# Stores of the split weights moved from SyncE's transfer queue to ScalarE's, placed by the order's model

## The chip, the cores and the metric

The kernel runs on one core of one Trainium2 chip. The metric is the device time of one execution in microseconds (us); lower is better. The core's engines are TensorE (PE, with its weight loads as PEld), VectorE (DVE), ScalarE (ACT), GpSimd (POOL) and SyncE (SP). Transfers between DRAM and the on-chip memory are issued by SP, ACT or POOL, each through a queue of its own; an issue appears as SPq, ACTq or POOLq in the profile. The transfers of all queues are carried by the core's 16 DMA engines.

## The reference

Two branches are computed from the same layer-normalised input and multiplied: attention over 2048 rows with 32 heads of width 18, and a bilinear gated feed-forward block of inner width 4608.

```python
x = A_x                                       # 1 x 2048 x 576
xn = _layernorm(x, axis=-1)
s = _A_ref(xn, A_wqkv, A_wo)                  # softmax attention, then @ wo
g = _silu(_B_ref(xn, B_w_gate, B_w_up, B_w_down))
...
# _B_ref: h = (x @ w_gate) * (x @ w_up); h @ w_down
```

The result is the product of s and g.

## The kernel before

The matmuls run in a 32-bit format of reduced precision (fp32r), so each operand is split in two: a high part, which is the value rounded to that format, and a low part, which is the rest. The terms that matter of the product of two split operands are added up in PSUM. Splitting the raw feed-forward weights is what this case is about.

The time has three parts. A prologue, to about 194 us, normalises the input, transposes it and makes queries, keys and values. The main loop, to about 2490 us, interleaves the feed-forward block with the attention, so that PE always has something to do. The tail makes the output projection and the product.

The feed-forward block goes over 72 units: 4 chunks of 512 rows (`c`), and for each 18 column blocks of 256 inner columns (`q`). A unit needs two tiles of up and gate weights (`wgu`, one for each n) and one of down weights (`wd`). In the first pass (c = 0, about 194 to 731 us) these tiles are made from raw weights. `g_raw` (L116) loads raw up and gate weights into `wraw`; three calls of `piece` copy the high part on ACT (L193) and subtract it on POOL (L194). `d_raw` (L124) and two calls of `dpiece` (L226 on ACT, L227 on POOL) do the same for the down weights. When a tile is done, `end` stores it to DRAM (`swg` at L199, `swd` at L232), and starts the raw load after next (wgu) or the next one (wd). Passes 2 to 4 load the split tiles from `swg` (L185) and `swd` (L220), in the opposite direction of columns in every other pass. One store of `swd`, at L216, belongs to the last column block and is made in the second pass.

A unit's up product is copied from PSUM on ACT (L680, `us`), multiplied with the gate product on DVE (L687) and split on ACT (L690, `hs`) and POOL (L691). The swapped halves of it are loaded as `hx` (L709), and L719 is the matmul with the down weights, added up on DVE (L747). The attention's scores are computed twice: L596 into the two banks `pa`, from which DVE takes the rows' maximum (L598), and L628 into the two banks `pb`, which ACT turns into exponentials (L630, `pt`). L639 multiplies them with the values. The heads' queries and keys come from DRAM as `pair` and `ring` (L245). The input's columns of the next chunk come as `xc` (L368, L371).

Instructions keep, on each engine and in each queue, the order in which the program issues them. In the main loop that order comes from a planner, `order()`. It keeps two clocks for PE (`clk`, one for each of two rows of PE), a time at which each other engine is free (`free`; `engine(eng, start, taken)` books a piece of work), and a model of the transfer queue (`moved()`). In each turn it takes the next matmul, score or other piece that can go. `small(now)` takes the next piece of split work from the list `chores` when the engine that it starts on is about free.

Of the kernel before, what the change touches and what calls it, by code (L numbers as in the profile page):

```python
# [20 lines left out]
FT = mybir.dt.float32  # L21
# [19 lines left out]
def kernel(  # L41
# [10 lines left out]
    nc = tc.nc  # L52
# [24 lines left out]
    swg = dram.tile([2 * NF2, 128, 18, 128], FT, name="swg")  # L77
    swd = dram.tile([NF2, 128, 2, 2, 2, HALF], FT, name="swd")
# [48 lines left out]
    def g_tile():  # L127
        return wpool.tile([128, 18, 128], FR, name="wgu", bufs=2)

    def d_tile():  # L130
        return wpool.tile([128, 2, 2, 2, HALF], FR, name="wd", bufs=1)
# [5 lines left out]
    def chore(all=True):  # L137
        q = (all and chores) or later
        if q:
            f, a = q.pop(0)  # L140
            f(*a)
# [5 lines left out]
    def ready(done, key):  # L147
        while key not in done:
            assert chores or later
            chore()  # L150
# [7 lines left out]
    def columns_of(u):  # L158
        c, q = units[u]
        return NF2 - 1 - q if c % 2 else q  # L160

    graw, gw, draw, dw = {}, {}, {}, {}
    gdone, ddone = set(), set()

    def g_load(n):
        if n < 2 * NF2:
            graw[n] = g_raw(n)

    def g_get(n):

        if n == 2 * len(units):
            u = n // 2 - 1
            dw[u] = wpool.tile([128, 2, 2, 2, HALF], FR, name="wdl", tag="wgu", bufs=2)
            nc.sync.dma_start(dw[u].bitcast(FT), swd[columns_of(u)])
            ddone.add(u)
        if n >= 2 * len(units):
            return
        f = 2 * columns_of(n // 2) + n % 2
        if n > 1 and n // 2 % NF2 == 0:
            gw[n] = gw[n - 2]  # L180
            gdone.add(n)
            return
        w = gw[n] = g_tile()
        if n >= 2 * NF2:
            nc.sync.dma_start(w.bitcast(FT), swg[f])  # L185
            gdone.add(n)
            return
        if n not in graw:
            ready(gdone, n - 2)
        raw = graw.pop(n)  # L190

        def piece(b):
            nc.scalar.activation(w[:, b:b + 3, :], raw[:, b:b + 3, :], AF.Copy)  # L193
            nc.gpsimd.tensor_tensor(w[:, 9 + b:12 + b, :], raw[:, b:b + 3, :], w[:, b:b + 3, :].bitcast(FT),  # L194
                                    op=OP.subtract)

        def end():
            gdone.add(n)
            nc.sync.dma_start(swg[f], w.bitcast(FT))  # L199
            g_load(n + 2)  # L200

        chores.extend([(piece, (b,)) for b in (0, 3, 6)] + [(end, ())])

    def d_load(n):
        if n < NF2:
            draw[n] = d_raw(n)

    def d_get(n):
        if n >= len(units) - 1:
            return  # L210
        p = columns_of(n)
        if n and n % NF2 == 0:
            dw[n] = dw[n - 1]
            ddone.add(n)
            if n == NF2:
                nc.sync.dma_start(swd[p], dw[n].bitcast(FT))  # L216
            return
        w = dw[n] = d_tile()
        if n >= NF2:
            nc.sync.dma_start(w.bitcast(FT), swd[p])  # L220
            ddone.add(n)
            return
        raw = draw.pop(n)

        def dpiece(k):
            nc.scalar.activation(w[:, k, :, 0, :], raw[:, k], AF.Copy)  # L226
            nc.gpsimd.tensor_tensor(w[:, k, :, 1, :], raw[:, k], w[:, k, :, 0, :].bitcast(FT), op=OP.subtract)  # L227

        def end():
            ddone.add(n)  # L230
            if p < NF2 - 1:
                nc.sync.dma_start(swd[p], w.bitcast(FT))  # L232
            d_load(n + 1)

        chores.extend([(dpiece, (k,)) for k in range(2)] + [(end, ())])
# [342 lines left out]
    with ExitStack() as mid:  # L578
# [225 lines left out]
        def begin():  # L804
            lo.extend(stk.tile([128, S], FR, name=f"o{k}", tag=tag) for k, tag in enumerate(("pair0", "pair1", "ring")))
            loads.extend((fetch_o, (k, c), 0.262) for c in range(2) for k in range(3))
# [86 lines left out]
        clk, free = [0.0, 0.0], {"DVE": 0.0, "ACT": 0.0, "POOL": 0.0}  # L893
# [10 lines left out]
        def engine(eng, start, taken):  # L904
            free[eng] = max(free[eng], start) + taken
            return free[eng] + TAIL[eng]
# [8 lines left out]
        def moved(start, size):  # L915

            queue[0] = max(queue[0], start) + size / 0.24
            return queue[0] + 2.0

        due, rows_done = [], {}  # L920
        there, queue = {}, [0.0]
        na = nb = 0
# [79 lines left out]
        def small(now):  # L1002

            q = chores or later
            if q and q is later and (now < quiet[0] or later[0][0].__name__ in ("second", "inverse") and nb < TOTAL):
                return
            if q:
                steps = KINDS.get(q[0][0].__name__, ())
                eng = steps[0][0] if steps else "POOL"
                if eng == "POOL" or free[eng] <= now + 0.1 + (0.15 * (now - quiet[0]) if q is later else 0.0):  # L1010
                    at = now
                    for eng, taken in steps:
                        at = engine(eng, at + 0.05, taken)
                    if not chores:
                        quiet[0] = now + PAUSES.get(q[0][0].__name__, 6.0)
                    chore()
# [93 lines left out]
        def order():  # L1110
# [5 lines left out]
            while any(heads) or na < TOTAL or nb < TOTAL or due:  # L1116
                now = max(clk)
                small(now)
                if nb == TOTAL and not lo:
                    begin()  # L1120
                if loads and queue[0] <= now + 0.3:
                    f, a, size_mb = loads.pop(0)
# [70 lines left out]

        heads, stuck, parts, loaded, stacks = [], [False], {}, {}, []
        order()


# [115 lines left out]
```

## Time and profile before

| What | Value |
|---|---|
| time of 3 runs, median | 2568.7 us |
| the three runs | 2567.2, 2568.7, 2570.92 us |
| profiled execution, its own time | 2567.59 us |
| profiled execution, span | 2565.8 us |
| mean clock granted to PE | 0.999 |
| PE / PEld busy | 2544.8 / 2106.5 us |
| DVE / ACT / POOL busy | 1931.5 / 1465.2 / 593.3 us |
| bytes moved by DMA | 504.58 MB, of which SP's queue (q1) 487.58 MB |

The span is the time between the first and the last instruction that the profiler saw; the execution's own time has 1.8 us beside it. Busy times are those in which the engine worked on at least one instruction. The profile names a group of instructions by its line in the kernel, its engine, its operation and what it writes and reads, as in `pt<-pb`. Where an engine was idle ahead of an instruction, "<-" gives what ended the wait.

### The profile page before, as it was taken

To read this page: it belongs to the slowest core of one execution; us is meant where nothing else is said; L and a number is where in the kernel's file an instruction comes from. 1 tells how busy PE (TensorE), PEld (TensorE's weight loads), DVE (VectorE), ACT (ScalarE), POOL (GpSimd) and SP (SyncE) were. 2 spreads that over 40 slices of the span, in tenths; PEclk is the share of its full clock that TensorE was granted. 3 is DMA by queue.
4 is the path that set the end of the run, shared out by engine and by line. 5 is a ranking of instruction groups with operands and counts; after the bars stand their busy time and mean duration, and the time that the engine had idled before them with its cause. 6 is when DMAs were issued, how large, how long until landed. Compare 5 with 4: busy or idle time off the path is not lost.

```text
span 2565.8 us, 59206 instructions
## 1 busy us (share of the span) xinstructions
PE 2544.8 (99%) x24360; PEld 2106.5 (82%) x24360; DVE 1931.5 (75%) x3377; ACT 1465.2 (57%) x2688; POOL 593.3 (23%) x663
## 2 busy tenths in 40 slices
PE   8999999999999999999999999999999999999999
PEld 7899888878878888878888888887888888878879
DVE  6208778777778898777778888777888887877537
ACT  5222666666756665655565666555665655555651
POOL 3214334433421111111111111111111111111125
PEclk9999999999999999999999999999999999999999
DMA  7799988888886666565676666665676666664577
GB/s 248 233 283 279 259 227 226 233 222 224 221 193 187 176 180 180 172 182 168 181 186 171 179 175 185 179 166 169 180 192 166 178 184 178 175 177 145 154 203 253
DMA packets 196058, 504.58 MB, mean 197 GB/s; under 512 B 58144, under 2 KB 116384, under 8 KB 156876
## 3 DMA queue, kind: packets, MB, share of 16 engines
q1 hardware_dynamic: 185100, 487.58, 68.2%
q0 software_dynamic: 9952, 11.74, 1.7%
q8 instruction: 192, 3.15, 0.6%
q10 hardware_dynamic: 736, 1.47, 0.2%
q14 instruction: 78, 0.64, 0.1%
HBM read 312.21 MB, written 107.61 MB: 164 GB/s over the span
## 4 chain that ended last, share of the span: by engine, by line
PE 97%; DVE 1%; DMA 1%; SPq 0%; issue 0%; ACT 0%; POOL 0%; DVEq 0%
PE pg L675 34%; PE pg L639 17%; PE pg L719 16%; PE pa L596 12%; PE pb L628 8%; PE pg L402 2%; PE pa L348 2%; PE pb L348 2%; PE pg L1243 1%; PE pa L1243 1%; PE pb L1243 1%; DMA hx<-hs 0%; DMA ring<-sqk 0%; DVE mx L598 0%; DMA xin<-in_A_x_dram 0%; DMA sot<-oc 0%
## 5 line engine op out<-in xcount | busy, mean ns | idle before, releaser
L598 DVE TENSOR_REDUCE mx<-pa 128x1 f32<-128x512 f32 x2048 | 1368.9, 687 | 226.1 <-PE pa L596 113.1
L630 ACT ACTIVATE pt<-pb 128x512 f32<-128x512 f32 x2048 | 1160.8, 597 | 538.2 <-PE pb L628 463.5
L675 PE MATMUL pg<-xc,wgu 64*128 64x512 f32 x7776 | 1363.9, 388 | 0.2 <-DVE acc L747 0.2
L675 PEld LDWEIGHTS pg<-xc,wgu 64*128 64x128 f32 x7776 | 1049.4, 184 | 41.4 <-DVE acc L747 0.5
L628 PE MATMUL pb<-pair,ring 64*128 64x512 f32 x2005 | 780.8, 395 | 2.3 <-DMA ring<-sqk 2.3
L596 PE MATMUL pa<-pair,ring 64*128 64x512 f32 x2006 | 777.3, 393 | 1.8 <-DVE mx L598 1.8
L719 PE MATMUL pg<-wd,hs 64*128 64x288 f32 x3408 | 585.1, 293 | 2.4 <-DVE acc L747 2.4
L719 PE MATMUL pg<-wd,hx 64*128 64x288 f32 x3360 | 572.4, 293 | 2.0 <-DMA hx<-hs 2.0
L719 PEld LDWEIGHTS pg<-wd,hs 64*128 64x128 f32 x3408 | 491.8, 185 | 7.1 <-DVE acc L747 2.8
L691 POOL TENSOR_TENSOR hs<-us,hs 128x512 fp32r<-128x512 f32 x144 | 185.9, 1291 | 1315.7 <-ACT hs L690 1301.6
L719 PEld LDWEIGHTS pg<-wd,hx 64*128 64x128 f32 x3360 | 480.4, 185 | 5.6 <-DMA hx<-hs 2.3
L639 PE MATMUL pg<-pt,vt 128*32 128x512 f32 x4096 | 455.8, 595 | 0.8 <-DVE acc L747 0.6
L596 PEld LDWEIGHTS pa<-pair,ring 64*128 64x128 f32 x2006 | 364.8, 184 | 70.7 <-issue 52.8
L628 PEld LDWEIGHTS pb<-pair,ring 64*128 64x128 f32 x2005 | 364.2, 184 | 9.3 <-issue 2.7
L639 PEld LDWEIGHTS pg<-pt,vt 128*32 128x32 f32 x4096 | 125.6, 110 | 285.1 <-issue 280.0
L747 DVE TENSOR_TENSOR acc<-acc,pg 128x288 f32<-128x288 f32 x544 | 234.0, 446 | 21.1 <-PE pg L719 20.1
L645 DVE TENSOR_TENSOR oc<-oc,pg 128x512 f32<-128x512 f32 x69 | 47.1, 683 | 216.6 <-PE pg L639 213.0
L690 ACT ACTIVATE hs<-us 128x512 fp32r<-128x512 f32 x144 | 91.0, 632 | 149.6 <-DVE us L687 148.0
L194 POOL TENSOR_TENSOR wgu<-wraw,wgu 128x384 fp32r<-128x384 f32 x108 | 108.4, 1015 | 97.3 <-ACT wgu L193 81.3
L643 ACT ACTIVATE oc<-pg 128x512 f32<-128x512 f32 x32 | 19.1, 598 | 184.9 <-PE pg L639 184.9
L687 DVE TENSOR_TENSOR us<-pg,us 128x512 f32<-128x512 f32 x144 | 98.4, 683 | 29.0 <-PE pg L675 22.3
L618 POOL DMA_DIRECT2D pair<-mt x128 | 77.6, 612 | 166.6 <-DVE mt L613 162.5
(143 smaller groups left out, 1366.5 us busy)
## 6 DMA issues: line engine op xcount, KB each, us to landing
wgu<-swg SPq DMA_DIRECT2D x102, 1152.0 KB
hx<-hs SPq DMA_DIRECT2D x140, 512.0 KB
wd<-swd SPq DMA_DIRECT2D x50, 1152.0 KB
swg<-wgu SPq DMA_DIRECT2D x36, 1152.0 KB
pair<-sqk SPq DMA_DIRECT2D x192, 144.0 KB
ring<-sqk SPq DMA_DIRECT2D x384, 72.0 KB
swd<-wd SPq DMA_DIRECT2D x18, 1152.0 KB
sqk<-hl SPq DMA_DIRECT2D x32, 512.0 KB
```

What stands on the lines that cost most here:

```text
L194: nc.gpsimd.tensor_tensor(w[:, 9 + b:12 + b, :], raw[:, b:b + 3, :], w[:, b:b + 3, :].bitcast(FT), op=OP.subtract)
L348: nc.tensor.matmul(p, wq[b, a], xcs[c][:, e, :], start=n == 0, stop=n == len(PAIRS) - 1)
L596: nc.tensor.matmul(p, q[rows, t * 128:(t + 1) * 128], k[rows, c * 512:(c + 1) * 512], start=True, stop=True)
L598: nc.vector.tensor_reduce(mx[h][:, t, c:c + 1], p, axis=AX.X, op=OP.max)
L628: nc.tensor.matmul(p, k[rows, t * 128:(t + 1) * 128], q[rows, c * 512:(c + 1) * 512], start=True, stop=True)
L630: nc.scalar.activation(pt[t, c], p, AF.Exp, scale=scale)
L639: nc.tensor.matmul(p[32 * c:32 * c + 32, :], vt[h // 2][:, t, 6 * (h % 2):6 * (h % 2) + 32], pt[t, c], start=t == ts[0], stop=t == ts[-1])
L675: nc.tensor.matmul(ps, gw[n][half[r], a, :], xg[i][half[r], e, :], start=k == 0, stop=k == len(TERMS) - 1)
L687: nc.vector.tensor_tensor(h32, ps, h32, op=OP.mult)
L691: nc.gpsimd.tensor_tensor(hj[:, 1, :], h32, hj[:, 0, :].bitcast(FT), op=OP.subtract)
L719: nc.tensor.matmul(ps[:, 0:HALF], (hx if k else hs)[u][half[r], j, a, s * 128:(s + 1) * 128], dw[u][half[r], k, j, e, :], start=n == 0, st ...
L747: nc.vector.tensor_tensor(a, a, ps[:, 0:HALF], op=OP.add)
```

## The change

The 53 stores of split tiles (36 of `swg`, 17 of `swd`, 1152 KB each) are no longer issued by SP at the place where the tile is finished. `end` puts them on a list, `saves`. At the head of each turn of `order()`, each new store gets a due time, the time at which the model has POOL free, plus 0.4 us; and when the first store of the list is due and ACT is nearly free in the model, ACT issues it, and the model books 0.5 us on ACT. The store at L216 stays on SP.

```diff
-    graw, gw, draw, dw = {}, {}, {}, {}
+    graw, gw, draw, dw, saves = {}, {}, {}, {}, []
...
         def end():
             gdone.add(n)
-            nc.sync.dma_start(swg[f], w.bitcast(FT))
+            saves.append((swg[f], w.bitcast(FT)))
             g_load(n + 2)
...
             if p < NF2 - 1:
-                nc.sync.dma_start(swd[p], w.bitcast(FT))
+                saves.append((swd[p], w.bitcast(FT)))
             d_load(n + 1)
...
+        save_at = []
...
             while any(heads) or na < TOTAL or nb < TOTAL or due:
                 now = max(clk)
                 small(now)
+                while len(save_at) < len(saves):
+                    save_at.append(free["POOL"] + 0.4)
+                if saves and save_at[0] + max(0.0, free["ACT"] - now - 0.1) <= now:
+                    save_at.pop(0)
+                    nc.scalar.dma_start(*saves.pop(0))
+                    engine("ACT", now, 0.5)
```

In the changed kernel the stores are at L1124. The following rows give the program's order on one engine: line, operation, what is written and read, the shape, and in brackets the semaphores that the row waits for. DMAHW0 to DMAHW7 are eight counters that the transfers of SP and ACT take in turn, in the order of the program; an issue waits on its counter until the transfer that took it before has landed.

ACT at the start of the main loop, before: the last copies of the prologue (`vo`), then the first unit's `us` and `hs`.

```order
L408 ACTIVATE vo_1164<-pg 128x16x18 [waits DMAHW0_49,PE_49]
L408 ACTIVATE vo_1164<-pg 128x16x18 [waits PE_49]
L680 ACTIVATE us<-pg 128x512 [waits PE_49]
L690 ACTIVATE hs<-us 128x512 [waits DVE_49]
L193 ACTIVATE wgu<-wraw 128x384 [waits DMAHW5_49,PE_49,Pool_49]
```

The same place now:

```order
L408 ACTIVATE vo_1164<-pg 128x16x18 [waits DMAHW7_49,PE_49]
L408 ACTIVATE vo_1164<-pg 128x16x18 [waits PE_49]
L1124 DMA swg<-wgu 128x2304 [waits DMAHW2_49,Pool_49]
L1124 DMA swd<-wd 128x2304 [waits DMAHW7_49,Pool_49]
L1124 DMA swg<-wgu 128x2304 [waits DMAHW2_49,Pool_49]
L680 ACTIVATE us<-pg 128x512 [waits PE_49]
L690 ACTIVATE hs<-us 128x512 [waits DVE_49]
L193 ACTIVATE wgu<-wraw 128x384 [waits DMAHW4_49,PE_49]
```

Three stores that SP issued during and right after the prologue stand together ahead of the first `us`; the third waits on the same counter, DMAHW2, that the first one takes, since that is used again between them.

ACT in a unit of the middle of the first pass (about 650 to 656 us before), before: exponentials (`pt`), the gate's copies, and the next split.

```order
L226 ACTIVATE wd<-draw 128x2x288 [waits DMAHW4_49,DMAHW2_49]
L630 ACTIVATE pt<-pb 128x512 [waits PE_49] x4
L680 ACTIVATE us<-pg 128x512 [waits PE_49,Pool_49]
L630 ACTIVATE pt<-pb 128x512 [waits PE_49] x4
L690 ACTIVATE hs<-us 128x512 [waits DVE_49]
L630 ACTIVATE pt<-pb 128x512 [waits PE_49]
L193 ACTIVATE wgu<-wraw 128x384 [waits DMAHW4_49,DMAHW5_49,DMAHW3_49,Pool_49]
```

The same place now:

```order
L226 ACTIVATE wd<-draw 128x2x288 [waits DMAHW4_49,DMAHW2_49]
L680 ACTIVATE us<-pg 128x512 [waits PE_49]
L630 ACTIVATE pt<-pb 128x512 [waits PE_49]
L1124 DMA swg<-wgu 128x2304 [waits DMAHW7_49,Pool_49]
L630 ACTIVATE pt<-pb 128x512 [waits PE_49] x2
L690 ACTIVATE hs<-us 128x512 [waits DVE_49]
L630 ACTIVATE pt<-pb 128x512 [waits PE_49] x2
L1124 DMA swd<-wd 128x2304 [waits DMAHW5_49,Pool_49]
L630 ACTIVATE pt<-pb 128x512 [waits PE_49] x2
L193 ACTIVATE wgu<-wraw 128x384 [waits DMAHW6_49,DMAHW0_49]
```

Two stores stand between exponentials, each with a wait for POOL and for a counter, and the exponentials are spread otherwise about `us` and `hs`.

SP at the same place, before: the raw loads, `hx`, and the stores among them.

```order
L199 DMA swg<-wgu 128x2304 [waits DMAHW1_49,Pool_49]
L116 DMA wraw<-in_B_w_up_dram 64x9x128 [waits DMAHW2_49]
L116 DMA wraw<-in_B_w_gate_dram 64x9x128 [waits DMAHW3_49]
L709 DMA hx<-hs 64x2048 [waits DMAHW4_49,PE_49]
L709 DMA hx<-hs 64x2048 [waits DMAHW5_49]
L232 DMA swd<-wd 128x2304 [waits DMAHW6_49,Pool_49]
L124 DMA draw<-in_B_w_down_dram 64x2x288 [waits DMAHW7_49]
```

The same place now:

```order
L709 DMA hx<-hs 64x2048 [waits DMAHW1_49,PE_49]
L709 DMA hx<-hs 64x2048 [waits DMAHW2_49]
L116 DMA wraw<-in_B_w_up_dram 64x9x128 [waits DMAHW3_49,Pool_49]
L116 DMA wraw<-in_B_w_gate_dram 64x9x128 [waits DMAHW4_49]
L124 DMA draw<-in_B_w_down_dram 64x2x288 [waits DMAHW5_49,Pool_49]
```

Both stores are gone from SP; their wait for POOL now stands on the raw loads behind them, and `hx` goes ahead of the raw loads here.

## The prediction

> **What bounds the kernel now.** I read the page's busy times first, then the chain that ended last, then the busy time by stage, and last the waits and the order of time on the engines that the change touches.
>
> ```profile
> span 2565.8 us, 59206 instructions
> PE 2544.8 (99%) x24360; PEld 2106.5 (82%) x24360; DVE 1931.5 (75%) x3377; ACT 1465.2 (57%) x2688; POOL 593.3 (23%) x663
> ...
> PE 97%; DVE 1%; DMA 1%; SPq 0%; issue 0%; ACT 0%; POOL 0%; DVEq 0%
> ```
>
> TensorE works for 99% of the span and carries 97% of the chain. The change removes no matmul, so its gain can only come out of the idle 21 us (2565.8 - 2544.8) and out of a clock below 1, and only where the stores run, in the first pass (194 to about 731 us). The table by stage shows where that pass loses time at all. Its columns are the window, its length, the busy time of PE, PEld, DVE, ACT and POOL with counts, the granted clock, the DMA share and GB/s.
>
> ```profile
> core 0: us, PE busy (x) PEld busy (x) DVE busy (x) ACT busy (x) POOL busy (x), PEclk, DMA share, GB/s
> ...
> 200.00:240.00 40.00, 40.00 (x369) 36.89 (x367) 36.90 (x62) 11.40 (x23) 19.71 (x18) 1.00 1.05 285
> 240.00:260.00 20.00, 19.23 (x204) 18.50 (x203) 18.71 (x34) 7.76 (x15) 12.46 (x13) 1.00 1.03 262
> 260.00:280.00 20.00, 17.96 (x157) 17.12 (x155) 12.40 (x21) 9.87 (x20) 6.98 (x6) 0.91 0.97 266
> ...
> 740.00:760.00 20.00, 17.72 (x145) 13.74 (x145) 13.65 (x22) 11.46 (x20) 6.55 (x7) 0.91 0.84 185
> ```
>
> Two stages stand out. In 260 to 280 us PE idles 20.00 - 17.96 = 2.04 us, and the clock of 0.91 takes another 0.09 x 20 = 1.8: 3.8 us. In 740 to 760 us it is 2.28 + 1.8 = 4.1 us. Together 7.9 us, 0.3% of the time, is nearly all that better transfers could win. What ended the two idle times stands in the waits of PE between 179 and 770 us (total, times, longest), and in the chains of these two stages and of the whole (start, us, what):
>
> ```profile
> PE pb L628 <- DMA ring<-sqk: 2.3, 1, 2.3
> PE pg L719 <- DMA hx<-hs: 2.0, 1, 2.0
> ```
>
> ```profile
> 1.66 4.47 DMA xin<-in_A_x_dram
> ...
> 263.62 10.87 DMA hx<-hs
> ...
> 745.33 10.38 DMA ring<-sqk
> ```
>
> Both are loads from SP's queue that were late: hx, issued at 263.62 us, landed 10.87 us later, and a ring load took 10.38, where the first transfer of the kernel, with nothing ahead of it, took 4.47.
>
> **The change, part by part.** SP loses 53 stores (36 of swg, 17 of swd). Their own time on SP, from the views of the two lines (least, median, longest ns, first and last start), and SP's waits in 179 to 770 us:
>
> ```profile
> L199 SPq DMA_DIRECT2D swg<-wgu x36: 326/343/3736, 153.4 to 705.5; - x36
> ```
>
> ```profile
> L232 SPq DMA_DIRECT2D swd<-wd x17: 326/1226/3704, 179.5 to 712.8; - x17
> ```
>
> ```profile
> SPq L199 <- POOL wgu L194: 97.8, 25, 10.6
> ...
> SPq L199 <- DMA swd<-wd: 11.2, 5, 3.3
> SPq L232 <- POOL wd L227: 9.8, 6, 2.3
> SPq L245 <- DMA draw<-in_B_w_down_dram: 7.9, 20, 1.1
> ```
>
> The issues free 36 x 0.343 + 17 x 1.226 = 33 us of SP's time, spread over 540 us. The 97.8 and 9.8 us that SP stood waiting for GpSimd are not won: in the new order the raw loads L116 and L124, which followed the stores, carry that wait themselves, since they overwrite the raw tile that GpSimd reads. So SP gets ahead by its issue times, and that counts only where a late load holds PE.
>
> Stall 1, hx at 263.62. SP's order there:
>
> ```profile
> 260.27 0.35 SPq L199 DMA_DIRECT2D swg<-wgu  x1
> ...
> 262.78 0.74 SPq L116 DMA_DIRECT2D wraw<-in_B_w_gate_dram  x1
> 263.62 2.28 SPq L709 DMA_DIRECT2D hx<-hs  x2
> 266.02 1.98 SPq L232 DMA_DIRECT2D swd<-wd  x1
> ```
>
> The swg store was issued 3.35 us ahead of hx in the same queue and leaves that queue. If hx then comes at least 2.0 us sooner, the stall goes, for -3.8 us. But the store's 1.18 MB go over the same 16 engines at the same time, and these are busy for 0.97 of the stage, so 0 is the other end; a loss I leave out here, as no new byte is added. Another queue beside SP's is in the trace: GpSimd's stores sot of 36 KB, and what each queue moved in the whole span:
>
> ```profile
> sot<-oc POOLq DMA_DIRECT2D x20, 36.0 KB, 6.1
> ```
>
> ```profile
> q10 hardware_dynamic: 736, 1.47, 0.2%
> ```
>
> From 284 to 715 us those stores land in a median of 6.1 us, well short of the 10.87 that hx takes behind SP's own backlog, so a second queue does not stand behind the first. I take -1.5, a little under the middle, for the share of 0.97. The Trainium skill, "DMA: Bandwidth & Descriptors", section "Queues, rings and completion order", says that each engine alternates between the queues that have work, a packet from one and then from the other. By it hx would gain nothing: in 10.87 us at 266 GB/s 2.9 MB pass, of which the store is 1.18; if the 1.7 MB of SP's queue alternate with the store's 1.18, all but some 0.5 MB are shared evenly, and the last byte of hx still lands after 2.9 MB. The sum would then be 1.5 us higher. The row of sot agrees with the alternation as such, but a small transfer is not hx, so I keep the middle.
>
> Stall 2, ring at 745.33. Ahead of it SP does, at the end of the pass:
>
> ```profile
> 712.80 1.23 SPq L232 DMA_DIRECT2D swd<-wd  x1
> ...
> 742.12 5.71 SPq L245 DMA_DIRECT2D ring<-sqk  x6
> ```
>
> The last moved store ends 28 us before the six ring loads start, and between them stand raw loads and the loads of the next chunk's xc, which stay. What SP gains is this issue, 1.23 us, and perhaps its wait. The ends are -4.1 (2.3 us sooner, the stall gone) and +0.5 (the loads meet other transfers); I take -1.0, the issue time, since PE is then held 1.2 us less, less a little for the transfer.
>
> ScalarE gets 53 issues. What one costs there is shown by the only transfers it issues now, L795; how its exponentials L630 stand to the matmuls L628, from the orders of time of ACT and PE:
>
> ```profile
> L795 ACTq DMA_DIRECT2D wor<-in_A_wo_dram x4: 388/446/1190, 2483.5 to 2485.7; - x4
> ```
>
> ```profile
> 2483.53 0.63 ACT L690 ACTIVATE hs<-us 128x512 fp32r<-128x512 f32 x1 [0.41 <-DVE us L687]
> 2483.53 2.59 ACTq L795 DMA_DIRECT2D wor<-in_A_wo_dram  x4
> ```
>
> ```profile
> 339.06 1.10 ACT L630 ACTIVATE pt<-pb 128x512 f32<-128x512 f32 x2
> ```
>
> ```profile
> 338.36 0.39 PE L628 MATMUL pb<-pair,ring 64*128 64x512 f32 x1
> ...
> 339.95 0.39 PE L628 MATMUL pb<-pair,ring 64*128 64x512 f32 x1
> ...
> 340.40 0.39 PE L628 MATMUL pb<-pair,ring 64*128 64x512 f32 x1
> ```
>
> There are two pb banks. The two exponentials end at about 339.63 and 340.16; the matmuls that take their banks again start at 339.95 and 340.40, so the slack is 0.24 to 0.32 us, and I use 0.3. What holds ACT for longer while an exponential is next holds PE by the rest. An issue of 0.446 is 0.15 beyond that, 53 x 0.15 = 8 us, if nothing covers it; but the issue starts with the ACTIVATE ahead of it (both 2483.53) whose 0.63 us covers it, and the order's model books 0.5 us on ACT for it. The other end of the issue time is SP's for the same stores: 36 x 0.04 + 17 x 0.93 = 17 us. I take a tenth of the 8, +0.75, range 0 to +17.
>
> The holds are the dearer part. A store on ACT waits for GpSimd's subtraction and, since all these transfers share eight counters in turn, for the transfer eight issues back. Queued behind it on ACT are exponentials (PE's pb banks), the split pieces L193 and L226 (GpSimd, then PE's weights) and the gate's copies L680 and L690 (DVE, GpSimd, then hx). GpSimd's end is booked with 0.4 us to spare, so I charge the counters. Nothing of the kind is on ACT today; the nearest rows are SP's. A typical one is L245 behind draw: 7.9 / 20 = 0.4 us, 0.1 beyond the slack. From 284 to 715 us, where exponentials run, there are 41 stores:
>
> ```profile
> swg<-wgu SPq DMA_DIRECT2D x27, 1152.0 KB
> swd<-wd SPq DMA_DIRECT2D x14, 1152.0 KB
> ```
>
> So 41 x 0.1 = 4, of which ACT's busy share of 57% meets work that is ready: +2.3. The low end is 0 (the transfer eight back has landed each time). The high end is the row of L199 behind swd, 11.2 / 5 = 2.24 us each, 1.94 beyond the slack; ten such are 19 us.
>
> At the loop's start three stores that SP issued from 153.4 us on wait until the loop begins and are issued together on ACT, and the third waits for the first to land. ACT's next work is
>
> ```profile
> 200.59 0.60 ACT L680 ACTIVATE us<-pg 128x512 f32<-128x512 f32 x1 [5.92 <-PE pg L675]
> ```
>
> ACT is free from 200.59 - 5.92 = 194.7. With a landing in 4.47 us (the least above) and an issue of 0.45 it is free again at 199.6 and nothing is late; with 10.87 at 206.0, and us, hs and the first hx come 5.4 us later. PE is busy for all of 200 to 240 us and has other columns to work on, so I take +1, from -1 (the stores no longer crowd the prologue's loads) to +5.
>
> Sum against the profiled execution of 2567.6 us (span 2565.8 and 1.8 around it): 2567.6 - 1.5 - 1.0 + 0.75 + 2.3 + 1.0 = 2569.2, say 2569.0. The median of the runs shown is 2568.7, 1.1 above the profiled one, and 0.2% of it, about what a measurement of this kernel can tell from no change, is 5.1 us.
>
> **The rivals.** A is the forecast: SP's 33 us were never on the path, the terms cancel, 2569.
>
> B, faster: both loads arrive in time, -3.8 and -4.1, and ACT's terms stay near 1: 2567.6 - 7.9 + 1 = 2561. For it: two stalls on late SP loads are all that PE lacks, and sot's 6.1 us. Against: stall 2 is 28 us past the last store, and the DMA share near stall 1 is 0.97.
>
> C, slower: ACT is held by the counters as SP was. Five of 36 stores waited 2.24 us each; of 53 it would be 7.4, so seven at 1.94 beyond the slack: +13.6, and 2567.6 - 2.5 + 0.75 + 1.0 + 13.6 = 2580. It decides when the holds beyond the slack pass about 7 us (5.1, the 1.1 between the profiled time and the median, and the 2.5 that the stalls give back, less 1.75 of the other terms), that is four such holds. For it: SP keeps its stock of ring, pair and raw loads in flight, so the one eight back is often only some microseconds old, and ACT had no such wait. Against: SP's five stood behind swd, which leaves SP's queue, and ACT is idle for 43% of the span.
>
> A further way, not a case of its own: the stores land later because ACT issues them later, and the next split L193 waits for its wgu tile. The next pass reads them from DRAM only after the raw loads of this one end, so only that tile counts, and it is within C.
>
> The Trainium skill, the same page, section "Issuing engines are not separate DMA queues", says that issuing from more engines saves only the sequencer's issue time. Case A says the same from the DMA share of 0.97, so it moves no chance.
>
> **How the numbers follow.** A 0.45, B 0.22, C 0.33: B can win at most 7.9 us and must win two thirds of it, C has the wider bounds. These are also the chances of within 0.2%, faster and slower. The likeliest is 2569.0, its own range 2563.6 to 2573.8. For 8 times in 10 the range takes in most of B (down to 2562) and of C (up to 2584, eight holds and an early stretch at +3); a tenth is left out above, where the 17 and 19 us ends meet, and less below.
>
> **What would show it.** In the profile after, q10 should move 1.47 + 53 x 1.18 = 64 MB, and the SP rows of L199 and L232 be gone. Stall 1: PE's wait for hx shrinks to below 1 us and the clock of 260 to 280 us is above 0.91. Stall 2: PE's wait for ring is still there, about a microsecond shorter. Holds: ACT's stores show times of 0.4 to 0.5 us, and waits behind DMA on ACT's queue of 5 to 15 us in sum; the idle time of PE L628 behind ACT, which has no row now, is 1 to 4 us. Start: L680 begins at 199 to 204 us. It would be wrong if L628 waits on ACT for more than 7 us, or if hx and ring both lose their rows and nothing takes their place.

## The result: slower by 0.7%, and the profile after

The changed kernel takes 2588.22 us (median of 5 runs, 2583.78 to 2591.56), the kernel before 2569.31 us (5 runs). The ratio is 1.0074, with a 95% interval of 1.0063 to 1.0086: 19 us slower, above the range of the prediction. The profiled execution of the changed kernel (span 2589.8 us) is one of its longer ones, 3.3 us above its median.

From the page of the changed kernel, busy times, queues, and the group of the matmuls that feed the exponentials:

```profile
PE 2555.4 (99%) x24360; PEld 2109.4 (81%) x24360; DVE 1929.9 (75%) x3377; ACT 1464.1 (57%) x2688; POOL 593.3 (23%) x663
...
q10 hardware_dynamic: 8368, 64.00, 6.6%
...
L628 PE MATMUL pb<-pair,ring 64*128 64x512 f32 x2005 | 782.4, 396 | 9.6 <-ACT pt L630 6.8
```

The change did what it says: ScalarE's queue q10 now moves 64.00 MB. New is the last row: L628 stands idle behind the exponentials of ACT for 6.8 us; before, its only idle time of 2.3 us was behind a ring load. The table by stage, with the columns of the one before:

```profile
200.00:220.00 20.00, 18.96 (x147) 15.93 (x144) 16.54 (x26) 5.01 (x10) 8.29 (x8) 1.00 0.89 315
...
260.00:280.00 20.00, 15.88 (x132) 14.76 (x130) 11.59 (x18) 10.31 (x18) 7.12 (x6) 0.95 1.06 274
280.00:300.00 20.00, 19.03 (x182) 17.63 (x182) 13.74 (x25) 10.64 (x20) 7.15 (x6) 0.87 0.96 255
...
560.00:580.00 20.00, 18.86 (x201) 17.11 (x199) 17.20 (x30) 16.06 (x32) 6.72 (x7) 1.00 0.72 225
...
600.00:620.00 20.00, 18.75 (x195) 12.88 (x192) 14.11 (x29) 10.99 (x21) 13.26 (x16) 1.00 0.48 152
...
660.00:680.00 20.00, 17.37 (x166) 15.30 (x163) 14.28 (x24) 12.97 (x26) 9.03 (x9) 0.91 0.78 238
680.00:700.00 20.00, 17.56 (x153) 11.88 (x154) 11.83 (x24) 8.08 (x15) 9.89 (x13) 0.91 0.60 171
...
760.00:780.00 20.00, 17.23 (x138) 12.87 (x139) 12.10 (x20) 10.38 (x18) 6.14 (x7) 0.91 0.85 187
```

Counted as in the prediction (idle time of PE, and the missing clock times 20 us), the lost time is:

| Stage, us | before | after | what PE waits for, after |
|---|---|---|---|
| 200 to 220 | 0 | 1.0 | L596 behind DVE |
| 260 to 300 | 3.8 | 8.7 | hx, then an exponential |
| 560 to 580 | 0 | 1.1 | an exponential |
| 600 to 620 | 0 | 1.3 | wd (GpSimd), mainly |
| 660 to 700 | 0.2 | 8.7 | two exponentials |
| 740 to 780 | 4.1 | 4.6 | ring |
| sum | 8.1 | 25.4 | |

The difference is 17.3 us. The medians are 19 us apart, but the two profiled executions counted here 24.0 (2591.56 and 2567.59), so the count places about 70% of it. Some 2 us more are lost from 800 to 2520 us, most of it in one spell of lower clock at 2514 us; the rest this count does not place. Both late loads are still there. PE's waits from 179 to 790 us:

```profile
PE pb L628 <- ACT pt L630: 6.8, 4, 2.6
PE pg L719 <- DMA hx<-hs: 4.1, 1, 4.1
PE pb L628 <- DMA ring<-sqk: 2.8, 1, 2.8
```

The four waits behind ACT end at 299, 564, 670 and 693 us. They take 6.8 us, and the lower clock of the stages 660 to 680 and 680 to 700 us takes 3.6 more: 10.4 of the 17.3 us. The late hx, with the clock behind it, takes 3.9 us more than before.

**What held the exponentials.** ACT's order of time around three stores (start, us; in brackets the idle time ahead and what ended it):

```profile
205.60 0.33 ACTq L1124 DMA_DIRECT2D swg<-wgu  x1
205.98 0.60 ACT L680 ACTIVATE us<-pg 128x512 f32<-128x512 f32 x1 [10.16 <-DMA swg<-wgu]
...
665.14 1.07 ACT L630 ACTIVATE pt<-pb 128x512 f32<-128x512 f32 x2
669.37 0.33 ACTq L1124 DMA_DIRECT2D swd<-wd  x1
669.75 1.08 ACT L630 ACTIVATE pt<-pb 128x512 f32<-128x512 f32 x2 [3.54 <-DMA draw<-in_B_w_down_dram]
...
688.07 1.08 ACT L630 ACTIVATE pt<-pb 128x512 f32<-128x512 f32 x2
692.37 0.33 ACTq L1124 DMA_DIRECT2D swg<-wgu  x1
692.74 2.28 ACT L630 ACTIVATE pt<-pb 128x512 f32<-128x512 f32 x4 [3.59 <-POOL wgu L194]
```

The first is the start, where the third store waits for the first to land. At 669 us ACT stands still for 3.5 us because the store's counter is held by a draw load, one of those which SP issued from 663.12 us on. At 692 us it waits for GpSimd's last subtraction, which was itself behind GpSimd's pair transfers, and these had waited for DVE (SP's order of time, then POOL's):

```profile
663.12 3.44 SPq L124 DMA_DIRECT2D draw<-in_B_w_down_dram  x4
```

```profile
688.78 2.54 POOL L618 DMA_DIRECT2D pair<-mt  x4 [2.78 <-DVE mt L613]
691.34 1.00 POOL L194 TENSOR_TENSOR wgu<-wraw,wgu 128x384 fp32r<-128x384 f32 x1
```

I laid each of the 53 stores beside the times at which its counter and GpSimd's count arrived in the trace. 13 were held for more than 0.3 us after the instruction ahead of them on ACT had ended: 7 by a counter (28.8 us together, the start's 9.3 among them), 6 by GpSimd (9.7 us). The other 40 were not held. At each of the 7 the store starts 0.07 or 0.08 us after its counter's transfer has landed. Only four of the 13, the stores at 298, 563, 669 and 692 us (three held by a counter, one by GpSimd, for 1.8 to 3.2 us), have a wait of L628 behind them. The three longest, 9.3 us at the start, 6.2 at 282 us and 4.8 at 234 us, have none.

The issue itself is cheap, for swd (326 ns in the median) as for swg:

```profile
L1124 ACTq DMA_DIRECT2D swg<-wgu x36: 326/327/382, 195.5 to 732.1; - x36
```

**What made hx later.** The two issues of hx on SP (least, median, longest ns, first and last start), before and after, the stores on ACT's queue, and the matmul that waited:

```profile
L709 SPq DMA_DIRECT2D hx<-hs x2: 596/1119/1642, 263.6 to 265.3; - x2
```

```profile
L709 SPq DMA_DIRECT2D hx<-hs x2: 708/2209/3710, 265.7 to 269.4; - x2
```

```profile
260.94 0.33 ACTq L1124 DMA_DIRECT2D swg<-wgu  x1
...
265.07 0.33 ACTq L1124 DMA_DIRECT2D swd<-wd  x1
```

```profile
279.54 0.60 PE L719 MATMUL pg<-wd,hx 64*128 64x288 f32 x1 [4.12 <-DMA hx<-hs]
```

hx is there at 279.5 us, 13.9 us after its issue at 265.67, against 10.87 before. That is 5.0 us later than before: 2.05 since it is issued later, 2.07 since SP needs 3.71 instead of 1.64 us for the first of the two issues, and 0.9 from the second issue to the landing. What lengthens the issue is not shown. On SP's queue one of the two stores, that of swd, stood behind hx (266.02 against 263.62 us); now it was issued 0.6 us ahead of hx on a queue of its own.

### The profile page after: what moved, and what is told of

Read it like the earlier page. It is cut to its first block, busy times and chain, and to the rows that moved or that the text cites. A ratio compares the mean times of both kernels' runs of the same rounds, so it can differ in the third digit from the quotient of the medians.

```text
span 2589.8 us, 59220 instructions
## 1 busy us (share of the span) xinstructions
PE 2555.4 (99%) x24360; PEld 2109.4 (81%) x24360; DVE 1929.9 (75%) x3377; ACT 1464.1 (57%) x2688; POOL 593.3 (23%) x663
## 4 chain that ended last, share of the span: by engine, by line
PE 71%; DVE 1%; DMA 0%; SPq 0%; issue 0%; ACT 0%; ACTq 0%
PE pg L675 26%; PE pg L639 14%; PE pg L719 13%; PE pa L596 9%; PE pb L628 7%; PE pg L1250 1%; PE pa L1250 1%; PE pb L1250 1%; DMA ring<-sqk 0%; DVE mx L598 0%; DVE mm L610 0%; SPq L245 0%; DVE us L687 0%; DVE acc L747 0%; DVE tp L655 0%
## 5 line engine op out<-in xcount | busy, mean ns | idle before, releaser
L628 PE MATMUL pb<-pair,ring 64*128 64x512 f32 x2005 | 782.4, 396 | 9.6 <-ACT pt L630 6.8
L596 PE MATMUL pa<-pair,ring 64*128 64x512 f32 x2006 | 779.2, 394 | 2.9 <-DVE mx L598 2.9
L596 PEld LDWEIGHTS pa<-pair,ring 64*128 64x128 f32 x2006 | 365.3, 185 | 72.7 <-issue 53.6
L628 PEld LDWEIGHTS pb<-pair,ring 64*128 64x128 f32 x2005 | 365.0, 185 | 19.0 <-ACT pt L630 10.4
```

Source lines behind the costliest of these rows:

```text
L596: nc.tensor.matmul(p, q[rows, t * 128:(t + 1) * 128], k[rows, c * 512:(c + 1) * 512], start=True, stop=True)
L628: nc.tensor.matmul(p, k[rows, t * 128:(t + 1) * 128], q[rows, c * 512:(c + 1) * 512], start=True, stop=True)
```

## The experiments

Two theories: *Hold*, with sharing (ScalarE is held by waits of its stores, and a store in a second queue slows hx), and *Order* (the chores moved by the planner and the 0.5 us booked on ACT make a worse order, whoever issues). Each run is compared with runs of the kernel before on the same chip.

**All stores back on SyncE, in the changed kernel's order.**

```diff
-                    nc.scalar.dma_start(*saves.pop(0))
+                    nc.sync.dma_start(*saves.pop(0))
```

> Every store is issued at the changed kernel's place of the program and the 0.5 us stays booked on ScalarE, but SyncE issues it; the matmuls' order is the changed kernel's, row for row. Theory Hold (ScalarE is held by its stores, about 9 us of lost matmul time, and hx is slowed by stores of a second queue, some 5 us with the clock): nearly all of the loss goes, 2567 to 2574 us, no idle time of L628 behind ScalarE. Theory Order (the moved chores and the booked 0.5 us make a worse order, whoever issues): 2583 to 2591 us, as the changed kernel.

Measured: 2571.03 us against 2568.76, ratio 1.0010 (1.0000 to 1.0019). No row of L628 behind ACT is left, nor one behind hx. PE still waits for the late ring, and for wd in the stage 600 to 620 us, which thus belongs to the order; two waits for loads of xc at 745 and 748 us, 1.5 us together, are new:

```profile
PE pb L628 <- DMA ring<-sqk: 1.8, 1, 1.8
...
PE pg L719 <- POOL wd L227: 1.0, 2, 0.5
```

The order accounts for at most 0.2%; the rest is that ScalarE issues the stores. Order has fallen as the main cause.

**The first three stores back on SyncE.**

```diff
-            saves.append((swg[f], w.bitcast(FT)))
+            if n < 2:
+                nc.sync.dma_start(swg[f], w.bitcast(FT))
+            else:
+                saves.append((swg[f], w.bitcast(FT)))
```

The store of swd has the same branch for n < 1.

> Only the first three stores (n = 0, d = 0, n = 1) go back to SyncE at their old place; the other 50 stay on ScalarE. Theory Hold, if the 10.2 us hold at the start is behind the late hx too: 1.4 us of the stage 200 to 240 us and the 4.8 us extra of the stage 260 to 300 us go, 2580 to 2583 us. If the hx stall comes from the stores beside it in the second queue: only the 1.4 us go, 2586 to 2588 us, and hx takes 12 to 14 us again. Theory Order: 2583 to 2591 us.

Measured: 2587.66 us, ratio 1.0082 (1.0065 to 1.0099). The 10 us hold at the start costs nothing that can be measured, and it is not behind the late hx:

```profile
PE pg L725 <- DMA hx<-hs: 5.0, 1, 5.0
```

(The branch moves the lines behind it by 6 in this and the next two kernels.)

**Only the first 14 stores on ScalarE, and only the other 39.** The branches are `n >= 10` and `n >= 4` (to SyncE) in the one kernel, `n < 10` and `n < 4` in the other.

> The first 14 stores (up to about 300 us) stay on ScalarE, the other 39 go back to SyncE. Theory Hold, from the lost matmul time by stage: 6.3 us of the loss lie before 300 us, so 2575 to 2578 us. Theory Order: no split by stage follows, the late part would keep its loss only with the booked time that goes with it.

Measured: 2572.65 us, ratio 1.0015 (1.0006 to 1.0024). PE's longest wait:

```profile
PE pg L725 <- DMA hx<-hs: 4.4, 2, 4.2
```

> The first 14 stores (up to about 300 us) go back to SyncE, the other 39 stay on ScalarE. Theory Hold: the 12 us lost from 560 to 700 us stay, in two to four waits of L628 on ScalarE, 2579 to 2584 us; where the holds fall is partly chance, since a store waits for the transfer eight back, so 2574 to 2584 us. If the early and the late part are independent, the losses of this run and of the run with the first 14 add up to 19 us within 5.

Measured: 2584.33 us, ratio 1.0066 (1.0051 to 1.0081), with

```profile
PE pb L634 <- ACT pt L636: 6.8, 4, 2.5
```

The two add up: 3.9 and 15.6 us are 19.5, against 18.9 for the whole change. The early part cost 3.9 where I expected 6 to 9. Four fifths of the loss come from the stores after 300 us. In the profile of that kernel 8.5 us of it are lost from 660 to 700 us, at the two waits on ACT there.

**Two stores of the 53 on SyncE, at the same place.**

```diff
-                    nc.scalar.dma_start(*saves.pop(0))
+                    k, *a = saves.pop(0)
+                    (nc.sync if k in (('d', 14), ('g', 33)) else nc.scalar).dma_start(*a)
```

> Two of the 53 stores, the one of swd for unit 14 and the one of swg for n = 33, are issued by SyncE at the same place of the program; all else, the booked 0.5 us too, is the changed kernel. These are the two that held ScalarE at 669 us (a counter taken by a draw load still on its way) and at 692 us (GpSimd's last subtraction behind its own pair transfers). Theory Hold: the two waits of L628 on ScalarE of 2.1 and 2.6 us go, and with them the lower clock of 0.91 in these stages, together 9 us: 2577 to 2582 us. Theory Order: 2584 to 2591 us.

Measured: 2580.61 us against 2568.45, ratio 1.0049 (1.0034 to 1.0064). It is 12.2 us above the kernel before, the changed kernel 18.9: 6.7 us less. The waits on ACT, and the two stages:

```profile
PE pb L628 <- ACT pt L630: 1.3, 2, 1.0
```

```profile
660.00:680.00 20.00, 20.00 (x204) 14.77 (x206) 15.87 (x27) 11.78 (x24) 11.29 (x13) 1.00 0.94 290
680.00:700.00 20.00, 19.60 (x188) 17.55 (x182) 17.44 (x32) 15.57 (x30) 8.09 (x9) 1.00 0.66 192
```

Two holds, one by a counter and one by GpSimd, together carried some 35% of the loss (the two intervals just touch, at 1.0063 and 1.0064); what each carries alone was not measured. In the changed kernel each of their stages had some 2.5 us of idle time and 1.8 of missing clock, 8.7 us in all, of which 0.4 are left.

**The two stores that ran beside hx on SyncE, behind hx.** The same edit with `('g', 7), ('d', 2)`.

> The stores of swg for n = 7 and of swd for unit 2 are issued by SyncE at the same place of the program, which is behind the hx loads on SyncE's queue; the other 51 stay on ScalarE. Theory Sharing (hx, issued at 265.67 us, took 13.83 us since these two stores ran beside it from ScalarE's queue): hx lands in 8 to 11 us, PE's wait for it falls from 4.1 us to below 1.5, the lost time from 260 to 300 us from 9.5 us to 3 to 5, and the run to 2582 to 2586 us. If hx is late since hs and the start are late: its time to landing stays near 13 us and the run at 2586 to 2591 us.

Measured: 2589.64 us, ratio 1.0083 (1.0068 to 1.0098): no gain, although the first half went as Sharing says. SP's order of time, the two stages, and ACT a little later:

```profile
262.94 1.22 SPq L709 DMA_DIRECT2D hx<-hs  x2
264.21 1.87 SPq L1125 DMA_DIRECT2D swg<-wgu  x1
```

```profile
260.00:280.00 20.00, 20.00 (x192) 19.10 (x190) 15.63 (x26) 13.62 (x25) 8.97 (x8) 1.00 1.04 247
280.00:300.00 20.00, 15.94 (x131) 13.57 (x130) 10.07 (x19) 8.30 (x16) 5.29 (x5) 0.83 0.97 311
```

```profile
288.54 0.33 ACTq L1125 DMA_DIRECT2D swg<-wgu  x1
288.91 0.60 ACT L630 ACTIVATE pt<-pb 128x512 f32<-128x512 f32 x1 [5.78 <-DMA pair<-sqk]
```

This hx is in time, and 260 to 280 us lose nothing (5.1 in the changed kernel). PE is then ahead of the next store, whose counter is held by a pair load, and ACT stands for 5.8 us: 280 to 300 us lose 7.5. The gain was given back within 10 us of time to the other mechanism. An earlier hx load, at 252 us, was 1.6 us late in this profile, and 1.7 in that of the two stores above, which up to there is the changed kernel's program; in the changed kernel's own profile it was in time. So a stage can differ by that much between single executions.

**More room for GpSimd.**

```diff
-                    save_at.append(free["POOL"] + 0.4)
+                    save_at.append(free["POOL"] + 3.4)
```

> Each store is due 3.4 us instead of 0.4 us after the time at which the model has GpSimd free; the order changes accordingly. If the waits for GpSimd carry much of the loss: the waits of ScalarE's stores for GpSimd fall below 1 us each, and the run is at 2575 to 2583 us. If the counters carry it: those waits are drawn anew, since each store then follows other transfers, 2580 to 2592 us, with one to three waits of L628 on ScalarE of 1 to 3 us.

Measured: 2609.88 us, ratio 1.0159 (1.0142 to 1.0176), 41 us slower than before and twice as bad as the change, beyond what I expected of either. PE's waits:

```profile
PE pb L628 <- ACT pt L630: 20.7, 8, 4.2
```

Laid out as above, one store is held by GpSimd (1.5 us), and 14 by counters (44.5 us). 12 of these 14 are stores of swd, and what holds their counters are hx, draw, ring and raw loads issued 5 to 13 us earlier, or a store before them. So waiting longer for GpSimd cures nearly all of its waits and makes the counters worse (the matmuls' order changes too, which this run does not set apart): what a store meets is set by which transfer was issued eight back, and how long ago.

**All stores on GpSimd's queue.** `nc.gpsimd.dma_start` in both `end`s; nothing is booked on ACT.

> The 53 stores are issued by GpSimd, right behind its own subtraction, at the place in the program where SyncE issued them; nothing is booked on ScalarE, so the matmuls' order is that of the kernel before. ScalarE can't be held by a store. Theory Hold: no wait of L628 on ScalarE; what is left is the sharing, hx in 12 to 15 us with 4 to 6 us of loss, and GpSimd's issue time of perhaps 1 us for each store: 2568 to 2578 us. If a second queue alone costs most of the loss, whichever engine holds it: 2580 us or more.

Measured: 2567.27 us, ratio 0.9994 (0.9984 to 1.0003). A store from POOL's order of time, hx, and the stage of the late ring:

```profile
260.28 0.60 POOL L199 DMA_DIRECT2D swg<-wgu  x1 [0.30 <-POOL wgu L194]
```

```profile
279.43 0.60 PE L719 MATMUL pg<-wd,hx 64*128 64x288 f32 x1 [4.60 <-DMA hx<-hs]
```

```profile
740.00:760.00 20.00, 20.00 (x202) 18.45 (x201) 18.54 (x36) 15.55 (x29) 7.54 (x8) 1.00 0.94 227
```

No wait of L628 on ACT is left, and with it the loss. Sharing stays: hx was issued at 264.04 us and is there 15.4 us later. Of this, 4.75 us go into the first of its two issues. The late ring is gone. In the sum this second queue costs nothing, but 260 to 300 us lose 4.2 us more than before and the ring's 4.1 us come back; why the ring is in time is not shown, so this balance is in part luck. In this trace GpSimd's transfers also take eight counters of their own, so the stores no longer stand among those of SP and ACT. ScalarE's queue costs the waits on ScalarE on top.

**Ten stores on SyncE at the same place, 43 on ScalarE.** The edit of the two stores, with swg for n = 1, 4, 7, 8, 33 and swd for units 2, 3, 4, 11, 14.

> Of the 53 stores of the changed kernel ten are issued by SyncE at the same place of the program: the eight that held ScalarE (swg for n = 1, 4, 8, 33 and swd for units 3, 4, 11, 14) and the two that ran beside the late hx (swg for n = 7, swd for unit 2). 43 stay on ScalarE, the matmuls' order and the booked time stay. Theory Hold with Sharing: what is left is the kernel with all stores on SyncE at these places, 2569 to 2575 us; 43 stores on ScalarE cost nothing. If each issue on ScalarE costs by itself (43 x 0.33 us, a third of it uncovered): 5 us or more above that, 2576 us and up.

Measured: 2575.45 us against 2569.06, ratio 1.0025 (1.0016 to 1.0034). Two short waits on ACT are left:

```profile
PE pb L628 <- ACT pt L630: 1.5, 2, 1.2
```

Ten stores carry 13 of the 19 us. The 6 us left are at the upper edge of Hold; all stores on SyncE at these places cost 2.3. Whether the 4 us between (whose intervals just overlap) are issues or new small holds stays open; its profile has these 1.5 us, and a ring load that is 3.0 us late against 1.8.

**All stores on SyncE, when due, nothing booked on ScalarE.**

```diff
-                if saves and save_at[0] + max(0.0, free["ACT"] - now - 0.1) <= now:
+                if saves and save_at[0] <= now:
                     save_at.pop(0)
-                    nc.scalar.dma_start(*saves.pop(0))
-                    engine("ACT", now, 0.5)
+                    nc.sync.dma_start(*saves.pop(0))
```

> All 53 stores are issued by SyncE, at the place where the model has GpSimd done plus 0.4 us; nothing is booked on ScalarE, so the matmuls' order is that of the kernel before. hx then stands ahead of two stores on SyncE's queue. If the queue's order alone is behind the first late hx: its lost time of 4.4 us falls to about 1 and the run to 2562 to 2567 us. If the gain is given back by later loads behind the later stores (as with all stores on SyncE at the changed kernel's places): 2567 to 2571 us.

Measured: 2562.25 us against 2569.06, ratio 0.9975 (0.9965 to 0.9985): faster than the kernel before. SP's order of time at the first late load, and the one wait for a load that PE has left in the pass:

```profile
261.86 1.70 SPq L709 DMA_DIRECT2D hx<-hs  x2
263.62 1.64 SPq L1124 DMA_DIRECT2D swg<-wgu  x1
```

```profile
PE pb L628 <- DMA ring<-sqk: 0.6, 1, 0.6
```

hx goes ahead of the store of swg that stood before it, and nothing waits for it.

**GpSimd's queue, but for five, and but for the first 14.** In both, the first three stores are issued by SyncE at the old place; then the stores of n = 7 and unit 2, or those of n < 10 and units below 4, go to SyncE when due, and the rest to GpSimd.

> The stores go to GpSimd's queue, but for five on SyncE: the first three at their old place, and those of n = 7 and unit 2 behind hx. Theory Sharing: the lost time from 260 to 300 us falls from 8.4 to about 2 us, the 2.3 us extra before 200 us go, and the late ring at 740 us stays away as with all stores on GpSimd's queue: 2558 to 2562 us. If the late hx and ring come back in other places: 2564 to 2570 us.

Measured: 2562.01 us, ratio 0.9972 (0.9961 to 0.9983).

> The first 14 stores are issued by SyncE (three at their old place, the rest when due), the other 39 by GpSimd. Theory Sharing: the first late hx is cured by SyncE's order and the late ring by GpSimd's queue, so 2558 to 2562 us; with one of them only, 2562 to 2566 us.

Measured: 2561.03 us, ratio 0.9967 (0.9956 to 0.9978), the fastest version here, 8.0 us below the kernel before. Both late loads are gone from its table:

```profile
260.00:280.00 20.00, 20.00 (x202) 19.22 (x200) 15.53 (x27) 13.64 (x26) 9.65 (x9) 1.00 1.01 298
...
740.00:760.00 20.00, 20.00 (x181) 14.47 (x180) 12.72 (x20) 10.49 (x19) 4.24 (x4) 1.00 0.49 131
```

The intervals of the three faster versions overlap, so their order among each other is not shown.

## Why the prediction was wrong, point by point

- **Holds, forecast +2.3, up to 19.** This is the step that failed most. The waits of L628 behind ACT take 6.8 us, and the clock after two of them 3.6: 10.4 us in the changed kernel's profile. Three things went wrong in the step. I charged a hold with the wait beyond the slack alone, while I had charged the two old stalls with the clock besides; the two holds at 669 and 692 us cost 6.7 us together, 3.4 on average, not 1.94. I took a mean of 0.4 us from twenty short waits, where 40 of 53 stores waited for less than 0.3 us and 13 for 0.6 to 9.3: four waits of L628 made the cost. And I said that GpSimd's end was booked with room; the model does not book GpSimd's own transfers, and one of the two dear holds was that. Rival C named the side and the counters, but not GpSimd; I gave it 0.33. Its price of 13.6 is not far from 10.4, in part by luck: it had seven holds and no clock, where there were four waits and 3.6 us of clock. My own sign of being wrong, L628 waiting on ACT for more than 7 us, did not quite show (6.8), since it too left out the clock. And the view of SP's waits that I priced the holds from has a dearer row, loads behind a store of swd, 2.9 us each, which I passed over:

```profile
SPq L245 <- DMA swd<-wd: 25.8, 9, 4.2
```

- **Stall 1, forecast -1.5, from -3.8 to 0.** Measured +4.9 in its stage, of which 1.0 is the wait of L628 at 298 us; the hx wait has 2.1 us more and the clock 1.8. I left out a loss "as no new byte is added". But the order in one queue had kept the store of swd behind hx, and a queue of its own set it beside hx: 13.9 us instead of 10.87 on ScalarE's queue, 15.4 on GpSimd's. The Trainium skill, "DMA: Bandwidth & Descriptors", section "Queues, rings and completion order", on alternating between queues, spoke against the gain. The trace agrees that there was none; but two thirds of the 3.0 us more lie in SP's issue, and no run here shows whether the alternation lengthens an issue.
- **Stall 2, forecast -1.0, from -4.1 to +0.5.** Measured +0.5 (4.6 against 4.1), at the upper end. SP's freed issue time did not reach the ring load. In the kernels with the stores on GpSimd's queue, or on SyncE when due, the ring came in time or 0.6 us late; in the one with all of them on SyncE in the changed order it was 1.8 us late. What decides it I have not settled.
- **The issues, forecast +0.75.** 0.33 us each, less than any row I used. With 43 of them left on ScalarE the kernel is some 4 us slower than with all of them on SyncE in the same order, so they cost at most about that; whether they do is open.
- **The start, forecast +1, us at 199 to 204 us.** It began at 205.98, at the long end that I had worked out (206.0). The cost was right or too high: 200 to 220 us lose 1.0 us, and without the hold the run is no faster.
- **Left out.** The order itself, with the booked 0.5 us, had no term in the sum; with all stores on SyncE it costs 2.3 us (ratio 1.0010, 1.0000 to 1.0019).
- **The ceiling of the gain, 7.9 us,** held: the best version takes away both stalls and gains 8.0 us.

## What to carry to other kernels

A transfer moved to a computing engine's queue makes that engine wait for whatever the issue waits for, in order with its work: ask of each issue which counter it needs and when the transfer that has it lands, and what else the engine that makes the data may be doing then. Two long waits on an engine with 0.3 us of slack cost more here (6.7 us) than the issues of 43 stores can have (some 4 us at most), and an idle time of over 2 us can bring a spell of lower clock that nearly doubles it. Where hx was issued ahead of both stores on SyncE's queue, it was in time (2562.25 us with all of them there when due): ahead of buying a second queue, put the load that is waited for before the store that nobody waits for.

## What was not expected of the hardware

The clock after a stall: three of PE's idle times, of 2.63 us (to 670.4 us), 2.04 (to 693.4) and 2.77 (to 775.9), went with a granted clock of 0.91 in their 20 us, 1.8 us more, while single idle times of 1.0 to 1.1 us left it at 1.00. Finer windows of the changed kernel, with the same columns, show what the 0.91 of 660 to 680 us is made of: half the clock for 3.4 us.

```profile
660.00:670.70 10.70, 8.07 (x72) 6.80 (x70) 7.40 (x12) 5.81 (x12) 4.30 (x4) 1.00 0.96 267
670.70:674.10 3.40, 3.40 (x19) 2.77 (x17) 1.38 (x2) 2.61 (x7) 2.01 (x2) 0.50 0.89 348
```

The Trainium skill, "TensorE: Matmul & The Clock Gate", section "Part 1: The HAM clock gate", says that the clock is halved after an idle window of about 3.4 us and is full again after one busy window. One window at half the clock would be 1.7 us, an estimate from that page, and the trace agrees; but here idle times shorter than the window were enough. They did not always do it: a single idle time of 2.51 us in the kernel with the two stores behind hx, and one of 2.81 us with swd 14 and swg 33 on SyncE, left the clock at 1.00 (the stages, in this order):

```profile
660.00:680.00 20.00, 17.49 (x178) 14.44 (x179) 15.67 (x27) 11.27 (x23) 8.46 (x8) 1.00 0.83 271
```

```profile
760.00:780.00 20.00, 17.19 (x166) 11.20 (x166) 10.00 (x17) 7.83 (x15) 1.29 (x1) 1.00 0.40 107
```
